# B and K turned by strided loads and VectorE, the decay's reciprocal taken channel-major, S and R S swapped between halves while they are copied

## The chip, the cores and the metric

The kernel runs on one core of one Trainium2 chip. A core has TensorE (PE), VectorE (DVE), ScalarE (ACT), GpSimd (POOL) and SyncE (SP); SP only issues DMAs here. The metric is the device time of one execution in microseconds (us); the median of three runs is compared. The profile is one execution taken with the hardware profiler.

## The reference

Two blocks are chained. The first is a linear recurrence with a 40 x 40 state for each of 4 batches and 8 heads over 768 tokens; the second is a mixture of four two-layer experts whose input is the first block's output.

```python
for t in range(S):                                   # B, H, S, D = 4, 8, 768, 40
    y[:, :, t] = np.einsum('bhd,bhde->bhe', rt, state)
    Sa = np.einsum('bhde,bhe->bhd', state, at)
    state_decay = state * wt[:, :, None, :] - np.einsum('bhd,bhe->bhde', Sa, bt)
    state = state_decay + np.einsum('bhd,bhe->bhde', vt, kt)
...
x = y.transpose(0, 2, 1, 3).reshape(B * S, H * D)    # 3072 x 320
p = domain_probs / (domain_probs.sum(-1, keepdims=True) + 1e-09)
for e in range(E):                                   # 4 experts, F = 1024
    out += p[:, e:e + 1] * (np.maximum(x @ w1[e], 0.0) @ w2[e])
```

## The kernel before

**Units.** The tokens are cut into 12 chunks of 64, the batches into two pairs, which makes 24 units (`NU`), a unit being 64 tokens of two batches and all 8 heads. A unit passes through `within` (all that needs no state), `substitute` and `merge` (the inverse of a unit triangular 64 x 64 matrix for each head), and `step` (what needs the state). Its output goes as `xT` into the mixture, which `mixture_of_chunk` computes for two units at a time: `up` (L718 to L742) multiplies by w1 and applies the ReLU, `add_h` (L827) forms the sums `a`, `down_1` and `down_2` multiply by w2 or by sums of its blocks, and `add` (L747) accumulates into `osb` with the gate.

**Two layouts.** Operands are needed by tokens (partitions are tokens, columns are heads x 40) and by channels (partitions are two heads x 64 slots, columns are tokens). There are two ways from one to the other. TensorE transposes four 128 x 128 blocks into a PSUM bank (`turn`, L331), and another engine copies the result out. Or the tensor is loaded a second time with a strided access pattern into a `raw` tile (`load_raw`, L188), and one VectorE transposition of 32 x 32 blocks finishes the turn (`turn_raw`, L221). Before the change W and A go the second way in every unit, R and V in units 3 to 23; in units 0 to 2 R and V are loaded into `padded` tiles and turned by TensorE. B and K are loaded by tokens only.

**`within` before.** Phase by phase (a phase ends at a `yield`): W is turned and its running product G taken by a scan (L397 to L405). TensorE turns G to tokens (`pg`, L411), VectorE multiplies it by W and takes the reciprocal of the 128 x 320 result (`gp`, L413 and L414). N = -B gp and K = K gp are formed by tokens (L450, L454), A is turned and multiplied by G (L456, L458), V and R are turned. Then TensorE turns N and K to channels and ScalarE copies them out (`turned`, L434 to L437). The causal scores `pc` follow, then `pfe` (the triangular matrix F, and E), then `pev`.

**`substitute` and `merge`.** F is gathered into `blocks` and transposed to M (L519); a chain of small operations on GpSimd (units 2 and later) or VectorE (units 0 and 1) solves for `Z` (L544, L557); `merge` turns Z into `Qc`, `QTc` and `QT`, with two TensorE groups `pY` and `pQ`.

**`step`.** `prn` (A times S, and S turned), `RH` (L621), `SN`, the copy of S turned (L626); `psat`; `pxr` (with R S), `RS`, the copy of R S (L667); `pdy` (new state and output); the output is stored into `xT` by 12 small DMAs. Half of the heads of R, V, S sit in the other half of the partitions (`d_half`, L352), so that S turned can be copied with two instructions over all 128 partitions.

**Order.** The program is written out by hand in a loop over units from L1021. `run(gen, n)` advances a generator by n phases, `gap(n)` inserts one or two pieces of the mixture. Inside one pass u of the loop are the step of unit u, the merge of u + 1, the `within` of u + 2 and the loads of u + 3. Each engine executes its own instructions in order; a scheduler sets that order ahead of time from the program order, the dependences and its own estimate of durations, so that an instruction can stand earlier in its engine's queue than in the program. `keep_in_program_order` (and `pin`, for units 0 to 3) forbids that for one instruction. Loads of R and V are kept in the list `later` and given out three to six at a time between pieces of the mixture (`begin_later`, L903). In the first passes `keep_warm` (L933) issues products on constants that nobody reads.

**Buffers.** `big` PSUM banks rotate by five, `mm` PSUM banks of the mixture by three; the tag `turned` has three buffers; each `raw` tile has one.

Of the kernel before, what the change touches and what calls it, by code (L numbers as in the profile page):

```python
# [15 lines left out]
def kernel(  # L16
# [43 lines left out]
    L = 64  # L60
# [87 lines left out]

    PADDED = 3
    padded = {}  # L150
    for n, a_sum in enumerate(("a1", "a7", "a5", "a2")):
        t = padded["RV"[n % 2], n // 2] = sb.tile([P, H, 64], FP32, name="padded", tag=a_sum)
        nc.gpsimd.memset(t[:, :, D:64], 0.0)
    raw = {x: kept(f"raw{x}", [P, 2 * NJ, 2 * D], 1, 0.0, nc.vector, D + D - Q) for x in "WARV"}
# [7 lines left out]
    RHs = kept("RH", of_64, 1, lo=D)  # L162
# [17 lines left out]
    def load(q, names):  # L180
        for x in names:
            q.n[x] = t = sb.tile([P, H, D], FP32, name=f"nat{x}", tag=f"nat{x}", bufs=2 if x in "WV" else 1)
            for i, bb in enumerate(q.b):
                nc.sync.dma_start(
                    out=t[i * L:(i + 1) * L], in_=srcs[x][bb, :, q.c * L:(q.c + 1) * L, :].rearrange("h t e -> t h e"),
                )

    def load_raw(q, names):  # L188


        moves = []
        for x in names:
            q.n["raw" + x] = t = raw[x]()
            heads = srcs[x].rearrange("b h t e -> (b h) t e")[q.b[0] * H:(q.b[1] + 1) * H, q.c * L:(q.c + 1) * L, :]
            heads = heads.rearrange("n (x two) e -> x n (two e)", two=2)
            for r in range(2):
                if x in "RV":

                    sets = ((slice(0, 8, 2), slice(r, 16, 4)), (slice(1, 8, 2), slice(3 - r, 16, 4)))
                else:  # L200
                    sets = ((slice(0, 8), slice(r, 16, 2)),)
                for n, hs in sets:
                    for y, w_ in enumerate((D + Q, 2 * D - Q)):
                        o = slice(64 * r + Q * y, 64 * r + Q * y + Q)
                        moves.append(lambda eng, out=t[o, n, 0:w_], in_=heads[:, hs, Q * y:Q * y + w_]: eng.dma_start(out=out, in_=in_))
        return moves

    def load_padded(q, x, eng=nc.sync):
        q.n["padded" + x] = t = padded[x, q.u % 2]
# [11 lines left out]
    def turn_raw(out, t):  # L221
# [3 lines left out]
            in_=t.rearrange("p n (two e) -> p n two e", two=2)[:, :, :, 0:Q],  # L225
# [7 lines left out]
    go(load_raw(units[0], "W"))  # L233
    load(units[0], "WBK")
    go(load_raw(units[0], "A"), nc.scalar)
    for x in "VR":
        load_padded(units[0], x, nc.scalar)
# [114 lines left out]
    def d_half(j, s):  # L352
        return s ^ (j % 2)

    def of_d_half(x, r):

        return x.rearrange("p (jj four) e -> p jj four e", four=4)[:, :, slice(1, 3) if r else slice(0, 4, 3), :]
# [19 lines left out]
    def causal(to, data):  # L377
        mask = mask_up[:, None, :].to_broadcast([P, data.shape[1], L])
        if len(to.shape) == 4:
            mask = mask_up[:, None, None, :].to_broadcast([P, 2, 2, L])  # L380
            data = data.rearrange("p (jj two) t -> p jj two t", two=2)
        return nc.vector.copy_predicated(out=to, mask=mask, data=data)

    def within(q):
# [20 lines left out]
        nc.vector.tensor_tensor(out=q.gl[:], in0=q.gl[:], in1=Gv[:, :, L - 1:L], op=ALU.mult)  # L405
        q.AT = sb.tile([P, 2 * NJ, L], FP32, name="AT", tag="AT", bufs=2)
        if q.u == 0:
            pin(turn_raw(q.AT[:], n["rawA"][:]))
        yield

        pg = by(turn("pg", tok(Gv), q.u == 2)[:], 64)[:, :, 0:D]  # L411
        gp = sb.tile([P, H, D], FP32, name="gp")
        pin(nc.vector.tensor_tensor(out=gp[:], in0=pg, in1=n["W"][:], op=ALU.mult))  # L413
        pin(nc.vector.reciprocal(out=gp[:], in_=gp[:]))  # L414

        def turn_rv():
            VT = sb.tile([P, 2 * NJ, L], FP32, name="VT", tag="turned", bufs=3)
            q.RT = sb.tile([P, 2 * NJ, L], FP32, name="RT", tag="RT", bufs=2)
            for x, t in (("V", VT), ("R", q.RT)):
                if q.u >= PADDED:  # L420
                    turn_raw(t[:], n["raw" + x][:])
                    continue
                p = turn(f"p{x}T", tok(n["padded" + x]), q.u == 1)[:].rearrange("p (j i t) -> p j i t", i=2, t=L)
                to = t[:].rearrange("p (i j) t -> p j i t", i=2)
                nc.scalar.copy(out=to[:, 0::2], in_=p[:, 0::2])
                for r in range(2):
                    nc.scalar.copy(out=to[half(r), 1::2], in_=p[half(1 - r), 1::2])
            return VT

        if q.u == 1:  # L430
            VT = turn_rv()
        yield

        def turned(name, x):  # L434
            t = sb.tile([P, NJ, P], FP32, name=name, tag="turned", bufs=3)
            nc.scalar.copy(out=t[:].rearrange("p j t -> p (j t)"), in_=turn("p" + name, tok(x), q.u == 1)[:])
            return t  # L437

        def token_V():
            return n["paddedV"][:, :, 0:D] if q.u < PADDED else n["V"][:]  # L440

        def causal_scores(VT):
            pc = quadrants(banks("pc"), 0, BY_TOKENS, L, lambda j, s, i: (
                d_half(j, s), i, j, of_slots(VT, d_half(j, s), j, i, D), of_slots(q.RT, d_half(j, s), j, i, D),
            ))
            for r in range(2):
                pin(causal(of_d_half(q.VC[:, :, D:D + L], r), pc[r]), q.start)

        q.K, q.N = k_tok(), n_tok()
        ins = nc.vector.scalar_tensor_tensor(  # L450
            out=q.N[:, :, 0:D], in0=n["B"][:], scalar=-1.0, in1=gp[:], op0=ALU.mult, op1=ALU.mult,
        )
        pin(ins)
        pin(nc.vector.tensor_tensor(out=q.K[:, :, 0:D], in0=n["K"][:], in1=gp[:], op=ALU.mult))  # L454
        if q.u > 0:
            pin(turn_raw(q.AT[:], n["rawA"][:]))  # L456
        at_ij = q.AT[:].rearrange("p (i j) t -> p i j t", i=2)
        ins = nc.vector.tensor_tensor(out=at_ij, in0=at_ij, in1=Gv.rearrange("p (j i) t -> p i j t", i=2), op=ALU.mult)  # L458
        pin(ins)
        q.VC = VCs()  # L460
        if q.u > 0:
            nc.scalar.copy(out=q.VC[:, :, 0:D], in_=token_V())
        if q.u >= PADDED:
            VT = turn_rv()
        yield

        NT = turned("NT", q.N)
        KT = turned("KT", q.K)
        yield

        if q.u > 0:
# [7 lines left out]
            s, i ^ s, j, of_slots(q.AT, s, j, i), of_pairs(NT, s, j, i),  # L479
        ))  # L480
        if q.u == 0:
            p = banks("pe")
        pe = quadrants(p, NJ * L, BY_TOKENS, L, lambda j, s, i: (
            s, i, j, of_pairs(KT, s, j, i), of_slots(q.AT, s, j, i),
        ))
        q.F = sb.tile([P, H, L], FP32, name="F", tag="F", bufs=2)
        for s in range(2):
            nc.scalar.copy(out=of_slot(q.F[:], s), in_=pf[s])
# [7 lines left out]
        if q.u == 0:  # L496
            tc.keep_in_program_order(nc.scalar.copy(out=q.VC[:, :, 0:D], in_=token_V()))
# [9 lines left out]
        if q.u == 0:  # L507
            causal_scores(turn_rv())
        yield
# [93 lines left out]
    def step(q, xT):  # L603
# [4 lines left out]
        if q.start:  # L608
            RH = q.EV
        else:  # L610
# [6 lines left out]
                s, d_half(j, s), 2 * i + j // 2, st[i][half(s), j, :], ident[half(s), half(s)],  # L617
            ))
            RH = RHs()
            for s in range(2):  # L620
                nc.vector.tensor_tensor(  # L621
                    out=of_slot(RH[:], s)[:, :, 0:D], in0=prh[s], in1=of_slot(q.EV[:], s)[:, :, 0:D], op=ALU.add,
                )
            SN = sb.tile([P, 2, 2 * 2, 64], FP32, name="SN", tag="step", bufs=3)
            for s in range(2):
                nc.scalar.copy(out=SN[:, s], in_=psn[s])  # L626
# [5 lines left out]
            i ^ s, d_half(j, s), j, RH[half(i ^ s), head(j, s), :], q.QT[half(i ^ s), head(j, s), :],  # L632
# [10 lines left out]
        if not q.end:  # L643
# [8 lines left out]
            d_half(j, s), i, j, SaT[half(d_half(j, s)), j, i ^ s, :], of_slots(q.RT, d_half(j, s), j, i),  # L652
        ))
        if not q.start:
            prs = quadrants(p, NJ * L, BY_PAIRS, L, lambda j, s, i: (
                d_half(j, s), s, 2 * (j // 2) + i, SN[half(d_half(j, s)), s, 2 * i + j // 2, :],
                of_slots(q.RT, d_half(j, s), j, i),
            ))
        for x in range(2):
            ins = causal(of_d_half(SX[:, :, D:D + L], x), px[x])  # L660
            if q.u == 0:
                tc.keep_in_program_order(ins)
        if not q.start:
            RS = sb.tile([P, NJ, 2, L], FP32, name="RS", tag="step", bufs=3)
            for x in range(2):
                for s in range(2):
                    nc.scalar.copy(  # L667
                        out=RS[half(s), x ^ s::2], in_=prs[x][half(s)].rearrange("p (j i) t -> p j i t", i=2),
# [275 lines left out]
    run(ws[0], 1)  # L944
    keep_warm(10)
    run(ws[0], 1)
    run(ws[1], 1)
    for x in "VR":
        load_padded(units[1], x)
    load(units[1], "WBK")  # L950
    go(load_raw(units[1], "A"))
    go(load_raw(units[2], "W"))
    load_probs()
    run(ws[0], 2)

    def scores_of_first():
        run(ws[0], 1)
        yield

    substitute(units[0], nc.vector, scores_of_first())  # L960
# [5 lines left out]
    load(units[2], "W")  # L966
    for x in "VR":
        load_padded(units[2], x)
    load_piece()
    load_piece()  # L970
    run(ws[1], 1)
    run(norm, 1)
    keep_warm(18)
    run(ws[1], 1)
    run(m)
    run(ws[2], 1)
    run(norm)
    load(units[2], "BK")
    go(load_raw(units[2], "A"))
    go(load_raw(begin(3), "W"))  # L980
    load_w2(0)
    load_piece()
    load_piece()
    load_w2(1)
    load_piece()
    run(s, 2)
    run(ws[1], 1)
    run(s)
    run(ws[1], 2)

    def scores_of_second():
        run(ws[1], 1)
# [126 lines left out]
```

## Time and profile before

| | |
|---|---|
| runs (us) | 1145.01, 1144.65, 1140.75; median 1144.65 |
| profiled execution | 1141.15 us, of which the span from first to last instruction is 1139.1 us |
| mean granted TensorE clock | 0.988 |
| PE busy | 1099.4 us (97%), 16036 matmuls |
| DVE busy | 757.8 us (67%) |
| ACT busy | 338.0 us (30%) |
| POOL busy | 473.6 us (42%) |
| DMA queue of SP | 265416 packets, 119.12 MB, 42.7% of 16 engines |

The span can be read in three stretches. The first 192 us hold the first units, in which little work of the mixture is at hand; TensorE is busy for 162.4 us of them. From 192 us to about 1010 us one unit follows another at an even pace. In the last 130 us there is only the mixture. A matmul's time in a listing runs from its start to the end of its pipeline, so that successive ones overlap; the cost of a group on TensorE is the distance between starts.

### The profile page before, as it was taken

To read this page: it belongs to the slowest core of one execution; us is meant where nothing else is said; L and a number is where in the kernel's file an instruction comes from. 1 tells how busy PE (TensorE), PEld (TensorE's weight loads), DVE (VectorE), ACT (ScalarE), POOL (GpSimd) and SP (SyncE) were. 2 spreads that over 40 slices of the span, in tenths; PEclk is the share of its full clock that TensorE was granted. 3 is DMA by queue.
4 is the path that set the end of the run, shared out by engine and by line. 5 is a ranking of instruction groups with operands and counts; after the bars stand their busy time and mean duration, and the time that the engine had idled before them with its cause. 6 is when DMAs were issued, how large, how long until landed. Compare 5 with 4: busy or idle time off the path is not lost.

```text
span 1139.1 us, 38245 instructions
## 1 busy us (share of the span) xinstructions
PE 1099.4 (97%) x16036; PEld 976.6 (86%) x16036; DVE 757.8 (67%) x1553; ACT 338.0 (30%) x860; POOL 473.6 (42%) x1221
## 2 busy tenths in 40 slices
PE   6899997999999999999999999999999999999998
PEld 5777776888998989889899898888989898888887
DVE  8756647697767768667677677677677586553343
ACT  2333333333233232332332332332332322311110
POOL 4005626662724635625526526437337246340000
PEclk8899998999999999999999999999999999999999
DMA  7784643254263454444453453443543442231330
GB/s 118 213 245 124 131 99 78 65 132 101 76 146 89 107 128 100 119 122 101 115 121 83 123 118 86 118 102 84 139 102 87 117 110 64 75 90 55 105 92 12
DMA packets 268867, 122.16 MB, mean 107 GB/s; under 512 B 213737, under 2 KB 242073, under 8 KB 268697
## 3 DMA queue, kind: packets, MB, share of 16 engines
q1 hardware_dynamic: 265416, 119.12, 42.7%
q8 instruction: 126, 2.06, 0.8%
q10 hardware_dynamic: 3280, 0.61, 0.3%
q14 instruction: 45, 0.36, 0.1%
HBM read 111.79 MB, written 3.93 MB: 102 GB/s over the span
## 4 chain that ended last, share of the span: by engine, by line
PE 87%; DVE 4%; SPq 2%; DMA 2%; POOL 2%; ACT 2%; issue 1%; DVEq 0%; ACTq 0%
PE ph L734 29%; PE p L841 28%; PE ph L726 9%; PE pdy L371 4%; PE pfe L371 2%; PE psat L371 2%; PE pxr L371 2%; PE prn L371 2%; PE po L775 2%; PE pQ L595 1%; PE pc L371 1%; PE pY L583 1%; PE pev L371 1%; POOL Z L557 1%; PE pg L335 1%
## 5 line engine op out<-in xcount | busy, mean ns | idle before, releaser
L734 PE MATMUL ph<-xT,w1p 128*128 128x256 f32 (+1 forms) x1520 | 344.1, 379 | 2.2 <-issue 2.2
L734 PEld LDWEIGHTS ph<-xT,w1p 128*128 128x128 f32 x1520 | 274.3, 190 | 65.1 <-issue 27.3
L544 POOL TENSOR_TENSOR Z<-M,Z 128x62 f32<-128x62 f32 (+7 forms) x352 | 143.3, 407 | 368.6 <-DVE M L535 336.0
L557 POOL TENSOR_TENSOR Z<-Z 128x31 f32<-128x31 f32 (+7 forms) x704 | 257.2, 365 | 55.2
L835 DVE TENSOR_TENSOR a<-hs 128x512 f32<-128x512 f32 x220 | 152.4, 710 | 128.2 <-ACT hs L739 128.2
L739 ACT ACTIVATE hs<-ph 128x512 f32<-128x512 f32 (+1 forms) x208 | 115.7, 564 | 295.5 <-PE ph L734 295.1
L841 PE MATMUL p<-sums,a 128*128 128x160 f32 x1056 | 165.1, 299 | 0.0
L752 DVE SCALAR_TENSOR_TENSOR osb<-p,gate,osb 128x320 f32<-128x320 f32 (+1 forms) x243 | 107.9, 481 | 74.9 <-PE p L841 70.9
L841 PEld LDWEIGHTS p<-sums,a 128*128 128x128 f32 x1056 | 152.9, 190 | 2.3
L726 PE MATMUL ph<-xT,w1p 64*128 64x256 f32 (+1 forms) x760 | 110.1, 398 | 1.2 <-issue 1.1
L841 PE MATMUL p<-w,hs 128*128 128x160 f32 x704 | 102.9, 299 | 0.0
L841 PE MATMUL p<-w,a 128*128 128x160 f32 x704 | 102.8, 299 | 0.0
L841 PEld LDWEIGHTS p<-w,hs 128*128 128x128 f32 x704 | 100.3, 190 | 2.2
L841 PEld LDWEIGHTS p<-w,a 128*128 128x128 f32 x704 | 98.0, 190 | 0.0
L576 POOL COPY QT<-QTc 32x256 f32<-32x256 f32 x96 | 51.6, 537 | 111.5 <-DVE QTc L570 103.7
L726 PEld LDWEIGHTS ph<-xT,w1p 64*128 64x128 f32 x760 | 67.8, 187 | 14.4 <-issue 4.4
L519 DVE STREAM_TRANSPOSE M<-blocks 128x1024 f32<-128x1024 f32 x24 | 47.0, 1957 | 23.1 <-ACT blocks L516 23.0
L414 DVE RECIPROCAL gp<-gp 128x320 f32<-128x320 f32 x24 | 51.7, 2152 | 0.8
L504 ACT COPY EV<-pev 64x160 f32<-64x160 f32 x96 | 23.4, 286 | 66.8 <-PE pev L371 66.3
L371 PE MATMUL pdy<-VC,k_tok 64*64 64x104 f32 (+1 forms) x768 | 41.6, 260 | 0.1
L600 ACT COPY QT<-pQ 32x256 f32<-32x256 f32 x48 | 17.4, 362 | 79.3 <-PE pQ L595 78.8
L626 ACT COPY SN<-prn 128x256 f32<-128x256 f32 x44 | 15.7, 370 | 84.1 <-DVE RH L621 81.9
(148 smaller groups left out, 1364.0 us busy)
## 6 DMA issues: line engine op xcount, KB each, us to landing
w1p<-in_moe_w_dram SPq DMA_DIRECT2D x95, 512.0 KB
w1p<-in_moe_w_dram SPq DMA_DIRECT2D x190, 64.0 KB
w<-in_moe_w_dram SPq DMA_DIRECT2D x4, 1280.0 KB
sums<-in_moe_w_dram SPq DMA_DIRECT2D x9, 512.0 KB
natW<-in_w_dram SPq DMA_DIRECT2D x48, 80.0 KB
natB<-in_b_dram SPq DMA_DIRECT2D x48, 80.0 KB
natK<-in_k_dram SPq DMA_DIRECT2D x48, 80.0 KB
out_dram<-osb SPq DMA_DIRECT2D x46, 80.0 KB
```

What stands on the lines that cost most here:

```text
L371: nc.tensor.matmul(out=p[row][half(col), lo + at * out_cols:lo + (at + 1) * out_cols], lhsT=lhsT, rhs=rhs, start=(n == 0), stop=(n == len( ...
L414: pin(nc.vector.reciprocal(out=gp[:], in_=gp[:]))
L519: ins = nc.vector.transpose(out=M[:], in_=cols)
L544: ins = eng.tensor_tensor(out=Z[:, 1:3, 0:n, j + 1:Q], in0=M[:, j:j + 2, None, j + 1:Q].to_broadcast([P, 2, n, m]), in1=Z[:, here, 0:n, j: ...
L557: eng.tensor_tensor(out=z[:, 0], in0=z[:, 0], in1=z[:, x], op=ALU.add)
L576: ins = nc.gpsimd.tensor_copy(out=q.QT[quarter(i), :, quarter(i % 2)], in_=QTc[quarter(i)])
L726: nc.tensor.matmul(out=ph[i][:, f, :], lhsT=w1.last[i * DT:(i + 1) * DT, f, :], rhs=xT[i * DT:(i + 1) * DT, 2, :], start=(f == 0), stop=False,
L734: nc.tensor.matmul(out=ph[i][:, f, :], lhsT=w1.main[:, g, at * P:(at + 1) * P], rhs=xT[:, g, :], start=False, stop=(g == 1 and f == HF // ...
L739: nc.scalar.activation(out=h[:, i * HF // 2:(i + 1) * HF // 2, 0:n], in_=ph[i][:], func=ACTF.Relu,)
L752: nc.vector.scalar_tensor_tensor(out=to, in0=p, scalar=sc, in1=to, op0=ALU.mult, op1=ALU.add)
L835: nc.vector.tensor_tensor(out=t[:], in0=x, in1=y, op=op)
L841: nc.tensor.matmul(out=p[:, n * HD:(n + 1) * HD], lhsT=a[:, f, :], rhs=b[:, f, :], start=(f == 0), stop=(f == HF - 1),)
```

## The change

B and K join the tensors that are loaded strided and turned by VectorE, in units 3 to 23; in units 0 to 2 all of A, B, K, R and V are loaded into `padded` tiles and turned by TensorE. W is no longer loaded by tokens. The reciprocal `rG` is taken of G by channels (504 columns shifted by one token and 8 last columns from `gl`, 512 in all, where it was 320); it multiplies B and K by channels on VectorE, and TensorE turns it to tokens, where VectorE multiplies B and K straight out of PSUM. The heads of R and V sit in their own half again; S and R S are swapped between halves by four copies of half the partitions each. F gets its sign on its copy out of PSUM. `RH` overwrites `EV`. The order in the loop and in the first units is rewritten, and 26 of the 44 `keep_warm` products are gone.

```diff
@@ load_raw @@
-                if x in "RV":
-                    sets = ((slice(0, 8, 2), slice(r, 16, 4)), (slice(1, 8, 2), slice(3 - r, 16, 4)))
-                ...
+                hs = slice(r, 16, 2)
+                for y, los, w_ in ((0, (0,), D + Q), (1, (0, D) if x == "W" else (0,), D - Q if x == "W" else 2 * D - Q)):
+                    o = slice(64 * r + Q * y, 64 * r + Q * y + Q)
+                    for lo in los:
+                        cols = slice(Q * y + lo, Q * y + lo + w_)
+                        moves.append(... eng.dma_start(out=t[o, :, lo:lo + w_], in_=heads[:, hs, cols]))
@@ within @@
-        pg = by(turn("pg", tok(Gv), q.u == 2)[:], 64)[:, :, 0:D]
-        gp = sb.tile([P, H, D], FP32, name="gp")
-        pin(nc.vector.tensor_tensor(out=gp[:], in0=pg, in1=n["W"][:], op=ALU.mult))
-        pin(nc.vector.reciprocal(out=gp[:], in_=gp[:]))
+        def by_channels(name, buf, n_bufs, x, factor=None):
+            t = sb.tile([P, 2 * NJ, L], FP32, name=name, tag=buf, bufs=n_bufs)
+            to = t[:].rearrange("p (i j) t -> p j i t", i=2)
+            if q.u < PADDED:
+                src = turn_padded(x)
+            else:
+                pin(turn_raw(t[:], n["raw" + x][:]))
+                src = to
+            if factor is not None:
+                factor = factor.rearrange("p (j i) t -> p j i t", i=2)
+                pin(nc.vector.tensor_tensor(out=to, in0=src, in1=factor, op=ALU.mult))
+            elif q.u < PADDED:
+                nc.scalar.copy(out=to, in_=src)
+            return t
+        rG = sb.tile([P, 2 * NJ, L], FP32, name="rG")
+        pin(nc.vector.reciprocal(out=rG[:, :, 0:L - 1], in_=Gv[:, :, 1:L]))
+        pin(nc.vector.reciprocal(out=rG[:, :, L - 1:L], in_=q.gl[:]))
+        yield
+        def by_tokens():
+            q.K, q.N = k_tok(), n_tok()
+            pg = by(turn("pg", tok(rG))[:], 64)[:, :, 0:D]
+            pin(nc.vector.scalar_tensor_tensor(
+                out=q.N[:, :, 0:D], in0=of_tokens("B"), scalar=-1.0, in1=pg, op0=ALU.mult, op1=ALU.mult,
+            ))
+            pin(nc.vector.tensor_tensor(out=q.K[:, :, 0:D], in0=of_tokens("K"), in1=pg, op=ALU.mult))
-        NT = turned("NT", q.N)
-        KT = turned("KT", q.K)
+        if q.u >= PADDED:
+            by_tokens()
+            yield
+        NT = by_channels("NT", "turned", 3, "B", rG[:])
+        q.AT = by_channels("AT", "AT", 2, "A", Gv)
+        KT = by_channels("KT", "turned", 3, "K", rG[:])
...
+        elif q.u < PADDED:
+            by_tokens()
@@ step @@
-            RH = RHs()
...
-                nc.scalar.copy(out=SN[:, s], in_=psn[s])
+                for x in range(2):
+                    nc.scalar.copy(out=SN[half(s), x ^ s::2], in_=psn[s][half(x)])
@@ first units @@
-    run(ws[0], 1)
-    keep_warm(10)
-    run(ws[0], 1)
+    run(ws[0], 2)
...
-    keep_warm(18)
+    keep_warm(2)
...
+    for x in "VRBAK":
+        load_padded(units[2], x)
+    load(units[3], "BKV")
+    go(load_raw(units[3], "ABKVR"))
@@ loop over units @@
+        run(w, 1)
         run(w_next)
         run(s, 1)
         gap(0)
...
         if u + 3 < NU:
-            go(load_raw(begin(u + 3), "WA"))
-            load(units[u + 3], "WBKV")
-            later.extend(load_raw(units[u + 3], "VR"))
-        run(w, 2)
+            go(load_raw(begin(u + 3), "W"))
+            load(units[u + 3], "BKV")
+            later.extend(load_raw(units[u + 3], "BAKVR"))
+        run(w, 1)
```

## The prediction

> **What bounds the kernel now.** I read the page first: busy times, slices, and the chain that ended last.
>
> ```profile
> PE 1099.4 (97%) x16036; PEld 976.6 (86%) x16036; DVE 757.8 (67%) x1553; ACT 338.0 (30%) x860; POOL 473.6 (42%) x1221
> PEclk8899998999999999999999999999999999999999
> PE 87%; DVE 4%; SPq 2%; DMA 2%; POOL 2%; ACT 2%; issue 1%; DVEq 0%; ACTq 0%
> ```
>
> The reader sees a kernel that TensorE's queue bounds, except at the left edge, where the granted clock dips. The windows view gives the stretches: 162.4 us of PE in the first 192 us, then 937 us in 947 us. So from 192 us on, a microsecond taken off PE is a microsecond off the time, unless something else becomes late. The timeline of PE shows what can be taken off (start, duration, operation):
>
> ```profile
> 614.68 1.25 PE L841 MATMUL p<-sums,a 128*128 128x160 f32 x8
> 615.77 0.60 PE L335 MATMUL pNT<-ident,n_tok 128*128 128x128 f32 x4
> 616.20 0.60 PE L335 MATMUL pKT<-ident,k_tok 128*128 128x128 f32 x4
> 616.73 0.69 PE L371 MATMUL pc<-RT,VT 40*64 40x64 f32 x32
> ...
> 626.80 1.25 PE L841 MATMUL p<-sums,a 128*128 128x160 f32 x8
> 627.98 0.69 PE L595 MATMUL pQ<-Yq,Qc 32*32 32x32 f32 x32
> ```
>
> pNT and pKT hold PE from 615.77 to 616.73, 0.96 us; what follows such a product without them starts 1.18 us after it (627.98 - 626.80), 0.09 later than pNT did (1.09). One unit gives back 0.87 us. A unit lasts 43.65 us (`gp` starts at 607.21 and 650.86).
>
> **PE's saving.** The two groups go in units 3 to 23: 21 x 0.87 = 18.3 us. At units 3 and 4 it isn't worth that: PE waits there 4.86 us, until 191.89, for QTc, whose chain (M at 163.57, 22 us of Z on POOL, Qc at 190.27) isn't shortened. I count 19 units, -16.5 us. The padded units 0 to 2 now turn six tensors on PE instead of five, 3 x 0.44 (pNT to pKT) = +1.3 us. The quadrant products keep number and columns; fewer rows (40 for 64) show no gain, since pc with 40 rows already takes 23 ns apiece and pfe with 64 takes 22. Their new order over quadrants I take as free, since pxr's two forms, which differ in it, take 24 and 20 ns.
>
> **VectorE, per unit.** Groups by shape (busy, then mean ns):
>
> ```profile
> L414 DVE RECIPROCAL gp<-gp 128x320 f32<-128x320 f32 x24 | 51.7, 2152 | 0.8
> L223 DVE STREAM_TRANSPOSE AT<-rawA 128x512 f32<-128x512 f32 x24 | 16.9, 704 | 5.1 <-DMA rawA<-in_a_dram 5.1
> L413 DVE TENSOR_TENSOR gp<-pg,natW 128x320 f32<-128x320 f32 x24 | 11.4, 476 | 0.5 <-PE pg L335 0.5
> ```
>
> The reciprocal of 24 columns (L311) takes 0.30 us, so a column costs (2.152 - 0.30) / 296 = 6.26 ns; 504 columns cost 3.30 and the 8 last ones 0.20. Added: 3.50, two turns at 0.70, two products at 0.70 (as L458's). Removed: 2.15 and 0.48. N and K from PSUM cost what L413 and the 0.54 of `osb` show, 1.02 for 1.09. Net +3.6 us, 76 us over 21 units. In the window 500 to 666 us DVE is busy 119.0 us of 166, 31.3 per unit; after, 34.9 of 42.8, 82%. That isn't a bound by itself; what matters is the one stretch where DVE has no slack:
>
> ```profile
> 642.24 0.71 DVE L223 STREAM_TRANSPOSE VT<-rawV 128x512 f32<-128x512 f32 x1 [1.03 <-DMA rawR<-in_r_dram]
> 645.78 1.43 DVE L835 TENSOR_TENSOR a<-hs 128x512 f32<-128x512 f32 x2 [2.82 <-ACT hs L739]
> ...
> 650.86 0.48 DVE L413 TENSOR_TENSOR gp<-pg,natW 128x320 f32<-128x320 f32 x1
> 651.37 2.15 DVE L414 RECIPROCAL gp<-gp 128x320 f32<-128x320 f32 x1
> ...
> 656.73 0.70 DVE L223 STREAM_TRANSPOSE RT<-rawR 128x512 f32<-128x512 f32 x1
> 658.84 0.63 DVE L568 STREAM_TRANSPOSE Qc<-Z 128x256 f32<-128x256 f32 x1 [1.41 <-POOL Z L557]
> ```
>
> RT is ready at 657.43 and pc starts at 660.41, so R's turn has 3.0 us of slack. After the change pc is due at 659.5. From 650.86 DVE has to do Y and the state (2.84), N and K (1.02), five turns and three products (8 x 0.70 = 5.6) before RT is ready: 660.3 if none ran earlier, 663.8 if the 3.5 us of rG stood there too. But DVE idles 5.9 us between 636.86 and 645.78, and V's turn, which the program has later, already sits in that gap. rG needs only G, and three of the eight need only loads: in the gap with them, RT ends at 658.2. So pc waits 0 to 4.3 us per unit; I take 0.1, as V's row shows the gap being used, +2 us over 20 units. Queued behind a late RT on DVE would be Qc, VC, G and `osb`; waiting for it, all of PE.
>
> **POOL's chain.** From pfe to QTc: QTc ends at 660.04, pY starts at 661.97, 1.9 us of slack, 1.06 after the saving. POOL's operations stretch under VectorE's products of two SBUF tiles:
>
> ```profile
> 644.56 0.77 POOL L557 TENSOR_TENSOR Z<-Z 128x76 f32<-128x76 f32 x2
> ...
> 645.92 1.48 POOL L557 TENSOR_TENSOR Z<-Z 128x68 f32<-128x68 f32 x2
> ```
>
> The second pair, smaller, ran beside two `a` sums: +0.37 us for each. Three more such products fall into Z's 22 us (NT, KT, and AT, now earlier), N and K leave that kind: about +0.6 us, inside the slack, cost nothing. The Trainium skill's "SBUF — State Buffer" (Who interferes with whom) calls the shared pair of ports an exclusive lock that blocks the later one wholly. By it three products hold POOL for 2.1 us less the 1.1 of N and K, and the slack would be just used up; the measured stretch is half of an operation.
>
> **ACT and the queues.** Two copies of 0.59 us go, SN takes four of 0.37 (RS's row) instead of two: -0.46 us on an engine busy 30%; SN is done at 623 and used at 639.75. SP issues 32 loads per unit before (4+4+8+8 raw, 8 by tokens) and after (6+20, 6), so no more issue time at 0.43 to 0.65 us each. Packets rise from 8192 to 9728 per unit, 12% of a share of 42.7%: at most 5 points, under PE. But `later` holds 20 moves instead of 16, and R's last two come behind the 12 stores of xT in the program, which took SP from 654.98 to 664.6. SP issued R's last one at 652.12, ahead of them; I take it that this stays.
>
> **Start-up.** To the first M (16.70 us) DVE's chain from the first scan grows by 0.9 us (3.5 for rG and three products from PSUM of 0.77, against 0.45, 2.15, 0.49, 0.48 and 0.77, with PE's and ACT's turns out of the way); six W loads over two queues instead of four on one give back up to 1 us. I count 0. Then 18 idle products hold PE from 32.5 to 38.5 while QTc is ready at 33.0: -5.5 us without them. But PE's granted clock was 0.50 from 20 to 36 us and 1.00 from 38 us, behind just these products. At half speed the chain's PE work up to 51 us (pY, pQ, psat, pdy, pxT, pc, pfe, 7.8 us) would cost up to as much again, +2.3 net. I take the middle, -1.5. By "TensorE: Matmul & The Clock Gate" (Part 1) some 3.4 us of sustained work bring full clock, and short bursts don't; the start-up term would then be +2.3 and the sum 3.8 us poorer.
>
> **Sum.** -16.5 + 1.3 + 2.0 + 0 - 1.5 = -14.7 us. The profiled execution took 1141.15 us (span 1139.1), 0.3% under the median; it would take 1126.5. From the median of 1144.65: 1130.
>
> **Rivals.** (1) VectorE becomes late at pc, and the kernel is slower. For: the stretch is full, and reciprocals and turns stand ahead of R's. Against: 8 us of DVE idle time per unit remain. Each microsecond of wait per unit costs 20 us, so it decides from 0.75 us on; at 2 us, between 0 and the 4.3 above, the time is 1130 - 2 + 40 = 1168. R's last load behind xT would show at the same place. Chance 0.20. (2) The saving is waited away at pY or pc: 0.4 to 0.8 us per unit, 1138 to 1146, within 0.5% (5.7 us, about what a measurement of this kernel can tell from no change). For: slack of 1.06 us and 1.3 us at these two. Chance 0.15. (3) Start-up also shortens: the full 5.5 us and the wait before 191.89 with its 8 us at half clock (4.9 + 4): 1130 - 4 - 9 = 1117. Chance 0.12. (4) PE turns no fewer tensors because unit by unit the turns return elsewhere: the code leaves pg alone in units 3 on, so I give it none. The forecast keeps 0.53.
>
> **How the numbers follow.** Faster: 0.53 + 0.12 = 0.65; same 0.15; slower 0.20. The forecast's own case runs from -18.3 - 5.5 + 1.3 = -22.5 (1122) to about 1138. The range reaches below it to 1114 for (3) with all 21 units, and above through (2) to 1152, which leaves out most of (1).
>
> **What would show it.** Right: no pNT and pKT, 512-column reciprocals near 3.3 us placed before `a`, PE busy nearly all of each unit, units 42.8 us apart, DVE near 830 us in all. Wrong: PE idle before pc with VectorE's RT as releaser, or before pY behind QTc; in the first 60 us a clock of 0.5 that lasts.

## The result and the profile after

The change made the kernel slower: 1287.3 us (median of 1285.56, 1290.97, 1283.5, 1289.02) against 1144.8, ratio 1.1253 [1.1208, 1.1297]. The forecast was 1130 with a range of 1114 to 1152.

The profiled execution took 1285.56 us. Its page answers the first lines shown of before:

```profile
PE 1200.6 (94%) x15828; PEld 1045.6 (81%) x15828; DVE 829.7 (65%) x1642; ACT 331.1 (26%) x844; POOL 475.2 (37%) x1226
PEclk7789987999797887997979899789797997899999
PE 75%; DVE 10%; SPq 7%; DMA 5%; issue 2%; ACT 1%; DVEq 0%; ACTq 0%
```

TensorE executes 208 matmuls fewer and is busy 101 us longer. The clock row says why: where before had a single digit under 9 behind the first two, dips now recur to the end. The mean granted clock fell from 0.988 to 0.887. As (1 - clock) x span this is 145 us of lost clock against 14 before, 131 us more, of the 145 that the span grew. VectorE (DVE) has a smaller share of a longer span, so it isn't the bound; but with SP's queue it has entered the chain.

PE's waits by releaser (us in total, times, longest). Before had no wait of pc for VectorE's RT. Behind this row come 13.0 us at pev, where before had 6.7:

```profile
PE pc L374 <- DVE RT L229: 39.0, 18, 3.2
```

The timeline of PE around one of the 18 (start, duration, operation, idle time before it):

```profile
490.29 1.25 PE L848 MATMUL p<-sums,a 128*128 128x160 f32 x8
493.70 0.69 PE L374 MATMUL pc<-RT,VT 40*64 40x64 f32 x32 [2.16 <-DVE RT L229]
...
495.69 1.06 PE L593 MATMUL pY<-QTc,F 32*32 32x32 f32 x32
...
503.88 1.22 PE L733 MATMUL ph<-xT,w1p 64*128 64x256 f32 x2
505.03 5.33 PE L741 MATMUL ph<-xT,w1p 128*128 128x256 f32 x16
```

pNT and pKT are gone, as forecast. But PE is idle for 2.16 us before pc, and what follows is slow: pY takes 1.06 us where it took 0.69, and sixteen products of a mixture piece 5.33 where they take 3.72. The windows view gives the granted clock in the same stretch (in each row PE's busy time leads, and the clock is the number before the last two):

```profile
489.00:492.00 3.00, 2.54 (x19) 2.29 (x17) 2.62 (x6) 0.00 (x0) 0.00 (x0) 1.00 0.84 242
...
495.00:498.00 3.00, 3.00 (x67) 2.64 (x62) 2.29 (x8) 1.77 (x5) 1.72 (x5) 0.50 0.74 124
...
507.00:510.00 3.00, 3.00 (x13) 2.52 (x12) 2.97 (x6) 0.60 (x1) 0.00 (x0) 0.78 0.00 0
```

From about 495 to 508 us PE runs without a pause at half speed. That happens once per unit: from 330 us on, the clock records hold 212 us of half clock in 16 stretches, behind 16 waits of pc. A unit, forecast at 42.8 us, takes 50 to 54.

Why RT is late is on VectorE and on SP. VectorE's timeline one unit later, and then SP's issues:

```profile
536.09 0.70 DVE L229 STREAM_TRANSPOSE VT<-rawV 128x512 f32<-128x512 f32 x1
539.92 1.29 DVE L842 TENSOR_TENSOR a<-hs 128x512 f32<-128x512 f32 x2 [3.13 <-ACT hs L746]
...
545.00 0.70 DVE L229 STREAM_TRANSPOSE RT<-rawR 128x512 f32<-128x512 f32 x1
```

```profile
527.98 0.98 SPq L210 DMA_DIRECT2D rawR<-in_r_dram  x2
529.06 8.93 SPq L718 DMA_DIRECT2D xT<-Y  x12
538.03 0.97 SPq L210 DMA_DIRECT2D rawR<-in_r_dram  x2
```

VectorE idles 3.13 us behind VT, then does the whole block of `a` and `osb` (left out of the listing), and only then RT, which waits for nothing when its turn comes. R's last two loads stand behind the 12 xT stores. The order of VectorE's queue is set ahead of time; the reading here is that, with R expected that late, RT was placed behind the block, and pc behind a second piece of the mixture.

### The profile page after: what moved, and what is told of

Read it like the earlier page. It is cut to its first block, busy times and chain, and to the rows that moved or that the text cites. A ratio compares the mean times of both kernels' runs of the same rounds, so it can differ in the third digit from the quotient of the medians.

```text
span 1283.8 us, 38036 instructions
## 1 busy us (share of the span) xinstructions
PE 1200.6 (94%) x15828; PEld 1045.6 (81%) x15828; DVE 829.7 (65%) x1642; ACT 331.1 (26%) x844; POOL 475.2 (37%) x1226
## 4 chain that ended last, share of the span: by engine, by line
PE 75%; DVE 10%; SPq 7%; DMA 5%; issue 2%; ACT 1%; DVEq 0%; ACTq 0%
PE ph L741 25%; PE p L848 20%; PE ph L733 9%; SPq L718 3%; PE pfe L374 3%; PE pdy L374 2%; PE psat L374 2%; PE prn L374 2%; DMA w1p<-in_moe_w_dram 2%; PE po L782 2%; SPq L210 2%; PE pxr L374 2%; PE pQ L605 2%; DVE osb L759 2%; PE pc L374 1%
## 5 line engine op out<-in xcount | busy, mean ns | idle before, releaser
L741 PE MATMUL ph<-xT,w1p 128*128 128x256 f32 (+1 forms) x1520 | 370.1, 400 | 0.0
L741 PEld LDWEIGHTS ph<-xT,w1p 128*128 128x128 f32 x1520 | 293.3, 203 | 74.6 <-issue 26.3
L554 POOL TENSOR_TENSOR Z<-M,Z 128x62 f32<-128x62 f32 (+7 forms) x352 | 156.0, 443 | 294.9 <-DVE M L545 258.6
L586 POOL COPY QT<-QTc 32x256 f32<-32x256 f32 x96 | 40.1, 418 | 326.7 <-DVE QTc L580 309.1
L733 PE MATMUL ph<-xT,w1p 64*128 64x256 f32 (+1 forms) x760 | 138.1, 442 | 0.6 <-ACT xT L710 0.6
L733 PEld LDWEIGHTS ph<-xT,w1p 64*128 64x128 f32 x760 | 79.5, 207 | 20.1 <-issue 6.3
L439 DVE RECIPROCAL rG<-G 128x504 f32<-128x504 f32 x24 | 79.1, 3296 | 0.0
L634 ACT COPY SN<-prn 64x256 f32<-64x256 f32 x88 | 32.2, 366 | 159.0 <-DVE EV L630 156.6
L374 PE MATMUL pc<-RT,VT 40*64 40x64 f32 x768 | 21.2, 264 | 40.4 <-DVE RT L229 39.0
L374 PEld LDWEIGHTS pc<-RT,VT 40*64 40x64 f32 x768 | 17.3, 168 | 46.7 <-DVE RT L229 43.6
L374 PE MATMUL pdy<-VC,k_tok 64*64 64x104 f32 (+1 forms) x768 | 43.6, 269 | 0.0
```

The lines of the kernel that those rows point to most:

```text
L374: nc.tensor.matmul(out=p[row][half(col), lo + at * out_cols:lo + (at + 1) * out_cols], lhsT=lhsT, rhs=rhs, start=(n == 0), stop=(n == len( ...
L439: pin(nc.vector.reciprocal(out=rG[:, :, 0:L - 1], in_=Gv[:, :, 1:L]))
L554: ins = eng.tensor_tensor(out=Z[:, 1:3, 0:n, j + 1:Q], in0=M[:, j:j + 2, None, j + 1:Q].to_broadcast([P, 2, n, m]), in1=Z[:, here, 0:n, j: ...
L586: ins = nc.gpsimd.tensor_copy(out=q.QT[quarter(i), :, quarter(i % 2)], in_=QTc[quarter(i)])
L733: nc.tensor.matmul(out=ph[i][:, f, :], lhsT=w1.last[i * DT:(i + 1) * DT, f, :], rhs=xT[i * DT:(i + 1) * DT, 2, :], start=(f == 0), stop=False,
L741: nc.tensor.matmul(out=ph[i][:, f, :], lhsT=w1.main[:, g, at * P:(at + 1) * P], rhs=xT[:, g, :], start=False, stop=(g == 1 and f == HF // ...
```

## The experiments

Theory T: R's two late loads put RT late, PE idles before pc, and each idle moment costs clock on top. Rival D: VectorE simply has too much to do. Rival G: the regrouped small products lower the clock by themselves. "Lost clock" below is (1 - mean granted clock) x span, in the one profiled execution of each kernel; half clock in the expectations is the length of the stretches at clock 0.50, twice the lost clock. The waits are totals of the whole execution.

| kernel | median us | ratio to before | lost clock | pc waits for RT | pY waits for QTc |
|---|---|---|---|---|---|
| before | 1144.8 | 1 | 14 | 0 | 6.5 |
| after | 1287.3 | 1.1253 [1.1208, 1.1297] | 145 | 39.0 | 3.5 |
| loads_5_8 | 1218.0 | 1.0657 [1.0627, 1.0688] | 70 | 20.7 | 26.2 |
| loads_5_10 | 1218.6 | 1.0660 [1.0635, 1.0685] | 84 | 27.9 | 23.6 |
| before_hold2 | 1268.3 | 1.1085 [1.1053, 1.1117] | 82 | 69.7 | 6.3 |
| fill18 | 1291.0 | 1.1252 [1.1179, 1.1324] | 65 | 0 | 7.1 |
| fill9 | 1233.0 | 1.0780 [1.0739, 1.0820] | 59 | 1.2 | 4.5 |
| fix_both | 1175.3 | 1.0268 [1.0212, 1.0325] | 56 | 28.0 | 3.3 |
| fix_both_warm | 1175.7 | 1.0296 [1.0266, 1.0326] | 37 | 28.0 | 1.6 |
| rg_after_M | 1283.8 | 1.1235 [1.1179, 1.1293] | 152 | 38.9 | 3.6 |
| before_recip | 1163.2 | 1.0183 [1.0151, 1.0216] | 23 | 0 | 11.0 |
| loads_7_10 | 1206.6 | 1.0578 [1.0540, 1.0615] | 63 | 7.3 | 46.1 |
| fix_710 | 1140.5 | 0.9966 [0.9942, 0.9990] | 34 | 7.5 | 6.1 |
| fix_710_warm | 1138.2 | 0.9957 [0.9940, 0.9974] | 28 | 7.7 | 4.9 |

**R's loads ahead of the stores.** The edit to the kernel after, and with 10 for 8 the second kernel:

```diff
-            begin_later(3 if n > 1 else 6)
+            begin_later(5 if n > 1 else 8)
```

> The change with one number moved: 5 and 8 of the waiting loads go out with each mixture piece instead of 3 and 6, so that all of R's loads stand ahead of the xT stores in SP's order. Theory T (R's last two loads behind the 12 xT stores put RT late on VectorE, PE waits 2.16 us before pc, and the clock halves behind each wait): from unit 9 on the waits before pc are under 0.3 us, the half clock falls from 293 us to under 120 us (what is left lies in the first 300 us, where units 1 to 7 keep their order), time 1125 to 1165. Rival D (VectorE's 3.6 us more per unit is the cause): PE still waits about 2 us before pc, time within 2% of 1287. Rival G (the regrouped small products pull the clock down by themselves): no waits before pc, yet over 200 us of half clock, time over 1220.

> As the 5 and 8 kernel, but 5 and 10: the order of PE in units 3 to 6 then comes back to that of the kernel before as well. Theory T: the waits before pc of 3.24 us at 204 us and 1.20 us at 282 us go too, and with them most of the half clock between 180 and 270 us (37 us of it, worth 18 us); time 5 to 25 us under the 5 and 8 kernel, 1115 to 1150. Rival S (the early loss of 15 us by unit 5 comes from the start-up, the idle products that were taken out and the padded transposes): no better than the 5 and 8 kernel within 4 us. Rivals D and G as there.

Both came to 1218: half of the loss is back, but the time lies in no theory's range. SP now issues all four of R's loads ahead of xT (from 494.19, xT from 505.97), and pc stands behind one piece of the mixture again. But pc still waits in every second unit (20.7 us, 9 times), and pY now waits too (26.2 us, 16 times). VectorE in `loads_5_8`, and PE:

```profile
486.40 3.29 DVE L439 RECIPROCAL rG<-G 128x504 f32<-128x504 f32 x1
489.61 1.87 DVE L529 STREAM_TRANSPOSE M<-blocks 128x1024 f32<-128x1024 f32 x1
...
516.36 0.61 DVE L578 STREAM_TRANSPOSE Qc<-Z 128x256 f32<-128x256 f32 x1 [6.12 <-POOL Z L567]
```

```profile
517.59 1.06 PE L593 MATMUL pY<-QTc,F 32*32 32x32 f32 x32 [3.19 <-DVE QTc L580]
```

The long reciprocal is done ahead of M, so POOL's substitution starts 3.3 us later and ends with VectorE waiting 6.12 us for it, which rules out D in this place. Theory T needs a second delay (T2): M behind the reciprocal. Rival S is not decided: `loads_5_10` is no faster, as S said, but pc's early waits, which that kernel was to take away, are still there (4.66 us at 192.19, 2.53 at 237.78, 2.31 at 278.83).

**The same two loads held back in the kernel before.**

```diff
-            begin_later(3 if n > 1 else 6)
+            begin_later(min(3 if n > 1 else 6, max(0, len(later) - 2)))
```

> The kernel before with nothing of the change, but with the last two loads of R held back until behind the 12 xT stores, as they stand in the kernel after. pc then comes behind the ups of a mixture piece. Theory T: PE waits 0.5 to 4 us before pc with RT as releaser in most units from unit 9 on, over 100 us of half clock, time 1190 to 1300. Should RT be there in time for pc in its later place, T says nothing is lost and the time is within 1% of 1145; the waits view decides which. Rival D (VectorE's load): within 1% of 1145 even if there are waits, which its lighter VectorE makes up. Rival G: within 1% of 1145.

1268.3. Here RT follows its load directly; VectorE waits for it and PE for VectorE, the top row of PE's waits:

```profile
631.71 0.71 DVE L223 STREAM_TRANSPOSE RT<-rawR 128x512 f32<-128x512 f32 x1 [6.09 <-DMA rawR<-in_r_dram]
```

```profile
PE pc L371 <- DVE RT L223: 69.7, 16, 5.0
```

Two loads in the wrong place cost a kernel that has nothing of the change 125 us. D and G fall as the whole cause.

**Useless work in the idle time.** The kernel after with products that nobody reads put in front of pc (18, then 9):

```diff
+            for _ in range(18 if q.u >= PADDED else 0):
+                warmer = n["rawR"][:].rearrange("p n e -> p (n e)")[:, 0:P]
+                nc.tensor.matmul(out=pcs[0][:, 0:P], lhsT=warmer, rhs=warmer, start=True, stop=True)
```

> The change with 18 products of 128x128 put in front of pc in each unit from unit 3 on (they multiply R's raw tile with itself into the place that pc overwrites); the order on all engines is otherwise that of the kernel after. They take about the time that PE is idle there, 2.2 us, so the wait itself is not won back, only the idleness. Theory T (the 131 us of the loss are the clock that drops behind the idle time, 39 us the idle time): the half clock after 330 us falls from 214 us to under 40 us, time about 1180 (1160 to 1205). Rival G (it is the order of small products and not the idle time that drops the clock): half clock over 150 us after 330 us, time 1280 to 1330. Rival D says the same as G: the time that RT is late is all that counts, so 1280 to 1300.

Time 1291, a miss for T and inside the ranges of G and D. The clock came out between T and G: the windows view of `fill18` has full clock from 280 to 540 us, one row of it being

```profile
330.00:400.00 70.00, 68.66 (x1042) 62.02 (x1044) 48.10 (x95) 17.81 (x45) 24.96 (x67) 1.00 0.43 105
```

From 547 us on it dips again: 68 us of half clock behind 330 us, where T had under 40 and G over 150. The profiled execution took 1276.06 us at a mean clock of 0.949; the other three, 1290 to 1296 us, had 0.930 to 0.936. The 18 products take 4.18 us, not 2.2, so from M of unit 8 to M of unit 12 a unit takes 48.6 to 50.2 us against 50.1 to 52.9 in the kernel after. Hence 9 in place of 18:

> As fill18, but 9 products in front of pc instead of 18: in fill18 the 18 took 4.18 us (0.232 us each) and so pushed pc 2.0 us behind RT; 9 take 2.09 us, just the 2.16 us that PE is idle there in the kernel after. They do no work that is wanted. Theory T: pc starts when it did, and PE's clock no longer drops behind it; of the 107 us that the half clock costs behind 330 us at least half comes back, time 1165 to 1235 (less if the waits of 0.4 to 1.3 us at pQ and psat, which took the clock in part of fill18's units, do so here too). Rival G (the order of the small products drops the clock): no change, 1275 to 1300, half clock behind 330 us as before, 214 us.

1233.0, at the upper end of T's range: useless work took 54 us off the kernel, and the half clock behind 330 us fell from 212 to 48 us. G falls as the main reason that the clock drops, since the small products stand in the same order. It doesn't fall altogether: the clock still drops six times there (nine in `fill18`), behind waits of 0.67 us at pQ (once 1.21 us at psat) with small products around them. One of the six, with the row of the windows view behind it:

```profile
483.23 0.24 PE L609 MATMUL pQ<-Yq,Qc 32*32 32x32 f32 x2 [0.67 <-ACT Yq L603]
484.00:494.00 10.00, 10.00 (x160) 8.22 (x155) 7.56 (x11) 4.47 (x13) 0.00 (x0) 0.51 0.29 70
```

What keeps a unit of `fill9` at 46.8 us and more, also where the clock is full, is only partly named: 2.09 us are the products, 0.67 a wait at pQ for ACT; over a microsecond stays open.

**Both delays.** `rg_after_M` is the kernel after with the first edit below, `fix_both` has 5 and 10 loads as well, `fix_both_warm` also the other two edits:

```diff
-        pin(nc.vector.reciprocal(out=rG[:, :, 0:L - 1], in_=Gv[:, :, 1:L]))
+        pin(nc.vector.reciprocal(out=rG[:, :, 0:L - 1], in_=Gv[:, :, 1:L]), True)
...
-    run(ws[0], 2)
+    run(ws[0], 1)
+    keep_warm(10)
+    run(ws[0], 1)
...
-    keep_warm(2)
+    keep_warm(18)
```

> The change with two edits of order and nothing else: 5 and 10 waiting loads go out with a mixture piece (R's loads ahead of the xT stores), and the 504-column reciprocal is held in program order, which puts it behind M on VectorE instead of ahead of it. Theory T2 (two delays, each ending in a PE wait: RT late because of R's loads; and, once that is mended, M late by the 3.3 us of the reciprocal, so that the substitution on POOL ends late and pY waits for QTc, 26 us in 16 waits in the 5 and 8 kernel): from unit 9 on no PE wait over 0.7 us, M to M 42.6 to 43.6 us, half clock under 90 us and all of it before 330 us, time 1140 (1122 to 1162). Rival D (VectorE has too much to do, whichever order): another wait of 1 to 3 us per unit appears, time over 1190. Rival P (pc's delay alone): no better than the 5 and 10 kernel, 1205 to 1225.

> As fix_both, and the idle products that the change took out of the start-up are back (10 before the second part of unit 0, 18 in place of 2 before the mixture begins). Theory T2 has no say here. If the lost products cost clock (the 5 and 10 kernel has 34 us of half clock in the first 60 us against 17 us before): 3 to 10 us under fix_both. If they only took PE time at the start (28 less 2 products of some 0.2 us): 1 to 6 us over it.

> The kernel after with the one edit that puts the 504-column reciprocal behind M; R's last loads stay behind the xT stores. Theory T2: RT still stands behind the sums and the osb block on VectorE, pc still waits about 2 us per unit, time 1265 to 1300. Rival M (the reciprocal ahead of M is the whole cause): waits before pc gone or under 0.5 us, time under 1200.

`fix_both` reached 1175.3, 13 us over T2's range and under that of P and D, and pY's waits are gone (26.2 to 3.3). Rival P falls; against T2's forecast stand 28 us of waits at pc, in every second unit. VectorE and PE in `fix_both_warm`:

```profile
625.28 1.59 DVE L759 SCALAR_TENSOR_TENSOR osb<-p,gate,osb 128x320 f32<-128x320 f32 x4 [1.77 <-PE p L848]
626.79 0.70 DVE L229 STREAM_TRANSPOSE RT<-rawR 128x512 f32<-128x512 f32 x1
```

```profile
627.54 0.64 PE L374 MATMUL pc<-RT,VT 40*64 40x64 f32 x28 [2.31 <-DVE RT L229]
```

VectorE sits idle for 1.77 us until a product lets `osb` go, with RT queued behind `osb` and PE waiting for RT: again place, not load. `rg_after_M` alone does nothing (1283.8), since in the kernel after the wait at pc hides M's delay. The idle products of the start-up changed nothing that this measures (1175.7 for 1175.3). The lost clock of these two, 56 and 37 us, can't be compared: the profiled execution of `fix_both_warm` took 1164.13 us at a mean clock of 0.968, the other four 1172 to 1179 at 0.955 to 0.960.

**The reciprocal's place alone.** The kernel before with one more reciprocal ahead of M:

```diff
+        if q.u > PADDED:
+            ins = nc.vector.reciprocal(out=M[:, 0:16, :], in_=q.G.rearrange("p c (x t) -> p (c x) t", t=Q))
+            tc.keep_in_program_order(ins)
```

> The kernel before, with one more reciprocal of 512 columns on VectorE in front of M in each unit from unit 4 on; its result is overwritten by M. The order on PE is that of the kernel before. Theory T2: M starts up to 3.3 us later, POOL's chain has about 1 us to spare, so pY waits 1 to 2.5 us per unit for QTc, over 100 us of half clock come with it, time 1190 to 1260. Rival H (the clock falls only through the change's other parts): pY waits 1 to 2.5 us but the clock stays, 1160 to 1190. Rival N (the delay is hidden): within 1% of 1143.

1163.2: under T2's range, and in H's, though with fewer waits at pY than either had (11.0 us, 7 times). VectorE's waits in the kernel before, from 330 to 1100 us, have this row, which the expectation had left out:

```profile
DVE M L519 <- ACT blocks L516: 22.3, 13, 3.3
```

VectorE idled 1.7 us ahead of M anyway, so by estimate M came about 1.6 us later, and in most units of the kernel before pY has 1.9 us of slack (QTc ends at 660.04, pY starts at 661.97). So the delay is mostly hidden here: from 330 us on pY waits three times, 4.5 us in all. Of the 20 us, 11.6 are lost by M of unit 8 (339.97 for 328.41). Behind it most units take 44.0 to 44.2 us for 43.6 or 43.7, which pY's waits don't account for; that stays open. VectorE's total, 819 us, is close to the 830 of the kernel after, at 1.8% instead of 12.5%: its load is not what matters.

**RT in its place.** As `fix_both` and `fix_both_warm`, with 7 and 10; `loads_7_10` has this edit alone:

```diff
-            begin_later(3 if n > 1 else 6)
+            begin_later(7 if n > 1 else 10)
```

> As fix_both, with 7 and 10 loads to a mixture piece: in fix_both RT stands behind four osb steps on VectorE in every second unit, which wait for a product of the mixture (pc waits 2.3 us there); with 7 and 10 it stands right behind VT in every unit from unit 6 on. Theory T2: no wait before pc over 0.3 us from unit 8 on, M to M 42.6 to 43.2 us in these units, time 1140 (1128 to 1158): the 28 us that fix_both loses between unit 8 and unit 23 are gone and 0.87 us per unit are won. Rival D (VectorE has too much to do in the stretch from M to pc): the wait moves on to pY, pg or pdy, M to M 44 us or more, time 1160 to 1185.

> As fix_710, with the start-up's idle products back. Both theories: within 6 us of fix_710, since fix_both_warm and fix_both stood at 1175.7 and 1175.3. Should the sign be the same here too, the start-up's idle products are worth nothing that this measures.

> The kernel after with 7 and 10 loads to a mixture piece and no other edit: the fourth corner beside the kernel after (3 and 6, reciprocal ahead of M: 1287 us), the one with M first alone (1284) and the one with both edits (1140.5). RT stands right behind VT, PE's order is that of the kernel with both edits, and M stands behind the reciprocal. Theory T2: no wait before pc from unit 8 on; M is 3.3 us later than with both edits, less VectorE's idle time there, so pY waits 1.5 to 3.2 us in most units, with half clock behind it: 1195 to 1230. Rival R (RT's place alone is what counts, and the reciprocal's only shifted idle time): within 8 us of 1140.5.

1140.5 and 1138.2: the change, with two edits of order, is level with the kernel before (0.3% to 0.4% ahead). The page of `fix_710`, and the longest row that is left of PE's waits from 330 to 1100 us (the next is 2.6 us at psat, with 2.5 in the kernel before):

```profile
PE 1088.0 (96%) x15828; PEld 963.6 (85%) x15828; DVE 828.1 (73%) x1642; ACT 329.3 (29%) x844; POOL 477.4 (42%) x1226
PEclk7698997989999999999999999999999999999999
```

```profile
PE pY L593 <- DVE QTc L580: 3.6, 6, 0.6
```

VectorE does the same work as in the kernel after (828 and 830 us) in 145 us less. The fourth corner, `loads_7_10`, came to 1206.6 with 46.1 us of waits at pY, as T2 had it; R falls. The four corners: with 3 and 6 loads 1287 and 1284 (reciprocal ahead of M, behind it), with 7 and 10 loads 1207 and 1140. The second delay costs 66 us, but only once the first is gone.

## Why the prediction was wrong

**The step that failed** is the last sentence on the queues: "SP issued R's last one at 652.12, ahead of them; I take it that this stays." It didn't: the text had seen that R's last two loads come behind the xT stores in the program, and took the executed order of the old program for that of the new one. With R's loads ahead of the stores and M ahead of the reciprocal, `fix_710` has no wait of pc from unit 8 on; `before_hold2` shows that two late loads are enough by themselves, in a kernel with nothing else of the change.

**VectorE's stretch.** "pc waits 0 to 4.3 us per unit; I take 0.1". It waited 2.16, within the bounds, but not for the reason that set them: the stretch was not full. VectorE idled 3.1 and 3.2 us in it, with RT queued behind work that wasn't ready. In `fix_710` all that was added fits, and from unit 8 on pc waits for nothing.

**Rival 1** named the event and its place, and even R's load behind xT. Its price, 20 us for each microsecond of wait per unit, was the mis-sized term: 39.0 us of waits came with 131 us of lost clock. It counted the wait and put the clock behind it at nothing. At 1168 for 2 us the range to 1152 had little of it; the measured price is some 70 us per microsecond (from M of unit 8 to M of unit 23 a unit takes 51.93 us for 43.70, 8.2 us more for a wait of 2.16, times 20 units).

**POOL's chain.** "inside the slack, cost nothing" weighed POOL's stretching and not M's start. rG was expected in VectorE's gap; its place ahead of M put 3.3 us on that chain, hidden in the kernel after and worth 66 us behind it. The chain itself grew by 0.8 us, where 0.6 of stretching was forecast (from the end of M's last product to Qc 21.98 us before, 636.86 to 658.84; 22.81 in `fix_710`, 642.07 to 664.88), and that is not inside the slack: pY waits 0.6 us in six units of `fix_710`.

**PE's saving** was right in kind. pNT and pKT took 0.96 us and are gone; from M of unit 8 to M of unit 23 a unit takes 43.70 us before and 43.30 in `fix_710`. 0.40 of the 0.87 arrive, 0.24 are lost in pY's remaining waits (3.6 us over 15 units), and 0.23 stay open. This is rival 2 in kind. That `fix_710` lies in its 1138 to 1146 is in part luck: the 6 us won between units 8 and 23 pay for a start-up loss that rival 2 didn't have.

**Start-up.** Forecast -1.5; in `fix_710` M of unit 7 comes 6.8 us later than before (290.48 for 283.73). The first M, counted as unchanged, is 1.8 us late (18.5 for 16.7). The mean granted clock is 0.72 in the first 60 us and 0.94 from 60 to 330 us, where it was 0.86 and 0.98: this was one of the signs named for being wrong. PE waits 4.91 us until 90.08 us for ET, where before waited 0.82 at 94.94; 4.74 us until 191.34 for RT only take the place of 4.86 until 191.89 for QTc. The idle products, which the forecast discussed, are little of it: with them M of unit 7 comes at 288.68. I didn't try any of this by itself, so the cause stays open.

**Right:** the long reciprocal (3.30 us forecast; below), VectorE's total (834 forecast, 829.7), pNT and pKT gone.

```profile
L439 DVE RECIPROCAL rG<-G 128x504 f32<-128x504 f32 x24 | 79.1, 3296 | 0.0
```

## What to carry to other kernels

When a change adds loads to a queue or work to an in-order engine, find the place that each new item gets in the executed order, since it isn't the old order with longer items; two small loads behind twelve stores cost 125 us in a kernel that has nothing else of the change. Price a wait of TensorE at the clock that follows it as well as at its length: from 330 us on, the two together came to four times the wait's length in the kernel after (34.5 us of waits at pc, 106 of lost clock), to about twice in `before_hold2` (69.7 and 61), and to one and a half times in `fix_both_warm` (18.4 and 10). When one wait is mended, look at once for the next, which it may have hidden.

## What was not expected of the hardware

In the kernel after, a wait of 2.16 us was enough to halve TensorE's clock, 16 times of 16 from 330 us on. The Trainium skill's "TensorE: Matmul & The Clock Gate" (Part 1) has the clock drop after an idle window of about 3.4 us; these waits are shorter, and the measurement decides.

But the length of the wait alone doesn't settle it. In `fix_both_warm` four of the eight waits of 2.3 us from 330 us on brought no half clock. One is the wait before 627.54 that is shown above; the clock stays at 1.00 behind it:

```profile
625.00:628.00 3.00, 0.69 (x30) 0.46 (x32) 2.72 (x6) 0.00 (x0) 1.07 (x5) 1.00 0.10 23
628.00:631.00 3.00, 3.00 (x122) 2.51 (x114) 1.66 (x5) 1.38 (x4) 1.97 (x5) 1.00 0.37 108
```

The clock records of all 14 traces show what differs. Within a trace the clock changes only at steps of a grid of 3.41 us, and every stretch of half clock between its two steps is a whole multiple of that (17.1, 13.7 or 3.4 us in the kernel after, from 330 us on). Counted from 60 us on over all traces, each of the 118 intervals between steps that began at full clock and held 2.0 us or more of PE's idle time was followed by half clock, and none of the 3901 that held under 0.6 us. In between it went both ways (54 of 241), so idle time isn't all that counts. The 2.16 us of the kernel after fell almost whole into one interval each time; the wait before 627.54 was cut by a step into 1.89 and 0.41 us. So what a wait costs depends on where it falls on this grid. The five executions of `fix_both_warm` had mean clocks from 0.955 to 0.968; that the grid is the reason is an inference, since only one of them was traced.

How long the clock stays low did not follow the wait's length. On the average 2.16 us of idle time bring 13 us of half clock in the kernel after (212 us in 16 stretches); in `before_hold2` 4.4 us (69.7 in 16) bring 8 (123 us in 16). There, the dense products of the mixture follow pc after 3.8 us (632.48 to 636.24), here after 10.2 (493.70 to 503.88), with small quadrant products and only six of the mixture's between them, and in both the clock is back 4 to 6 us after the dense ones begin. In `before_hold2`:

```profile
632.48 1.14 PE L371 MATMUL pc<-RT,VT 40*64 40x64 f32 x32 [4.63 <-DVE RT L223]
...
636.24 3.78 PE L734 MATMUL ph<-xT,w1p 128*128 128x256 f32 x8
```

```profile
641.00:644.00 3.00, 3.00 (x21) 3.00 (x20) 1.91 (x4) 0.00 (x0) 0.00 (x0) 0.87 0.75 235
```

This fits rival G in part: without idle time the small products never dropped the clock here, but they may keep it down, and they stand around the 0.67 us that dropped it in `fill9`. No run changes that alone, so it is argued, not shown.
